# Moving PSUM copies from VectorE to ScalarE in the first eight head pairs, and the decay table's trip through DRAM to the front of the queue

## The chip, the cores and the metric

The kernel runs on one core of a Trainium2 chip. The core has five engines that run side by side and wait for each other by semaphores: TensorE (PE: matrix products and transposes, results in PSUM), VectorE (DVE), ScalarE (ACT), GpSimd (POOL) and SyncE (SP, which here only issues DMAs). The metric is device microseconds per execution. Before the change the median of three runs is 807.27 us (802.27 to 809.57).

## The reference, cut to what matters

Two blocks follow each other. The first is causal attention with a decay over 64 heads (8 batches of 8) of 576 tokens and 64 channels. The second takes the heads' outputs side by side as `x` (8 x 576 x 512) through a gated network whose gate mixes tokens.

```python
log_f = np.log(np.clip(f, 0.0001, 1.0))
cum = np.cumsum(log_f, axis=-1)
decay = cum[:, :, :, None] - cum[:, :, None, :]
scores = np.where(causal, -1000000000.0, scale * q @ k.T + decay)
attn = softmax(scores)              # max taken off, sum + 1e-9
x = heads side by side of attn @ v

h = np.maximum(x @ w_in, 0.0)       # u, v are its two halves
v_n = (v - mu) / np.sqrt(var + 1e-06)
v_s = np.einsum('ts,bsd->btd', w_spatial, v_n) + b_spatial[None, :, None]
out = (u * v_s) @ w_out
```

## The kernel before

The work is cut by pairs of heads: 32 pairs, four to a batch (`PPB`). The tokens of a pair are four blocks of 128 and a tail of 64. One pair goes through these steps:

- `prep` (L218) loads q and k (`qk_t`) and the pair's decay rows (`dk` for the four blocks, `dt` for the tail), and GpSimd writes the causal mask into the latter. The decay rows come from a table, `rows_d`, in DRAM: `decay_rows` (L72) computes the table `rt` once at the start for all heads and writes it out at L86; the loads at L229 and L230 read one row of it into all partitions. `prep_v` (L243) loads v.
- `scores` (L263) and `scores_tail` (L302) let TensorE multiply q by k into PSUM banks `sc`, VectorE subtract the decay and take the row minimum of the negated scores (L260, `lowest`, result `nm`), ScalarE take the exponential with the row sum (L291 and L317), VectorE invert the sum (L294, L295) and GpSimd scale the row (L299, L320). The result is the attention matrix, in `tt` and `tl`; odd pairs of the first batch have tiles of their own, `t`, `d`, `d2t`.
- `transposes` (L344) and `transposes_tail` (L356) transpose its blocks on TensorE (L350, L362) into PSUM tiles `tp`. `evac` (L340) copies each finished `tp` to `e` in SBUF: ten copies to a pair, of which every other one is VectorE's. A counter, `nev`, decides: per pair ScalarE takes four 512 or 256 wide and one of the two tail copies, VectorE takes two of 384, two of 128 and the other tail copy (384).
- `attend` (L370) multiplies `e` by v: 28 products in one piece (L378), which wait for all ten copies. ScalarE rounds the result to `xh` (L387), VectorE keeps the remainder `xl` (L388). L417 copies the last 64 columns of `xl` behind those of `xh`.

While pair P is transposed, pair P+1 is scored: the generator `attention` (L394) interleaves them. `load_first` (L130) splits half of w_in, w_spatial and b_spatial into high and low parts at the same time, with 13 DMAs and work on VectorE, ScalarE and GpSimd; `load64` (L112) is the chain for the weights: `w` loaded, ACT L118, DVE L119, L121, L122, L124, L125, POOL L126, ACT L127, POOL L128. The rest of the weights (`load_rest`, L158) is split inside the first batch's network. `moe` (L431) is the network of one batch: its products are recorded under L214. From the first network on, the main loop (L569 to L577) interleaves the network of a batch with the attention of the next batch.

The order on each engine is not the order of the code: the framework's scheduler rearranges all instructions by its own forecast, within the data dependencies. `after` (L107) adds an ordering edge to that: a DMA is queued on SP behind a marked instruction, without waiting for its end. Before the change the w_in chunks stand behind the first q/k load, and w_spatial and b_spatial behind ScalarE's rounding of the first pair's result (L387), where that is already recorded.

## Time and profile before

| | |
|---|---|
| median of three runs | 807.27 us |
| the profiled execution | 811.62 us, span 809.4 us |
| TensorE busy | 770.3 us (95%) |
| VectorE, ScalarE, GpSimd busy | 444.0, 406.9, 385.6 us |
| mean granted TensorE clock | 0.978 |
| DMA, mean | 98 GB/s |

A row of the timeline gives start and duration, engine, source line, operation, output and input, and in brackets the idle time before it and what ended that. A row of a group gives the count, the total and the mean duration. A window gives the busy time of every engine in a stretch and the clock that was granted to TensorE there (1.00 is full). The 2.2 us between span and execution lie outside the instructions.

### The profile page before, as it was taken

What the parts mean: (1) busy time and instruction counts of PE and PEld (TensorE: products, weight loads), DVE (VectorE), ACT (ScalarE), POOL (GpSimd) and SP (SyncE); (2) the same over time, 40 slices, a digit from 0 to 9 for tenths busy, and PEclk for the clock granted to TensorE, in tenths of its full rate; (3) what the DMA queues carried; (4) which work ended last, traced back from release to release, by engine and by line L of the source; (5) the groups of instructions that cost most, each with busy time, mean ns of one, the idle gap of its engine ahead of it and who ended that gap; (6) DMA issues with size and microseconds to landing.
All of it is one profiled execution on the core that took longest, in us unless ns stands there. A gap on an engine that the chain in (4) does not pass through costs nothing.

```text
span 809.4 us, 14544 instructions
## 1 busy us (share of the span) xinstructions
PE 770.3 (95%) x4933; PEld 608.0 (75%) x4934; DVE 444.0 (55%) x1502; ACT 406.9 (50%) x1100; POOL 385.6 (48%) x713
## 2 busy tenths in 40 slices
PE   8679879899999989999999999999999999999997
PEld 3246668687887867878788877877788877878896
DVE  7866798844654535555564545445454436543322
ACT  3656566554655445555564455544564436542331
POOL 5854676754734236444452437443544435433231
PEclk9879999899999999999999999999999999999999
DMA  8553432434222233333321342222333333201001
GB/s 262 178 158 118 144 131 84 119 108 121 95 95 92 53 112 95 95 108 96 115 92 40 103 134 96 95 92 54 98 95 95 121 105 97 65 27 44 27 1 66
DMA packets 34764, 79.43 MB, mean 98 GB/s; under 512 B 4225, under 2 KB 8321, under 8 KB 34690
## 3 DMA queue, kind: packets, MB, share of 16 engines
q1 hardware_dynamic: 34370, 77.98, 31.2%
q8 instruction: 39, 0.64, 0.4%
q10 hardware_dynamic: 320, 0.52, 0.2%
q14 instruction: 35, 0.29, 0.1%
HBM read 68.73 MB, written 9.75 MB: 97 GB/s over the span
## 4 chain that ended last, share of the span: by engine, by line
PE 71%; DMA 4%; ACT 2%; issue 1%; POOL 1%; DVE 1%; SPq 0%; ACTq 0%; POOLq 0%
PE ps L214 41%; PE sc L378 7%; PE sc L278 7%; PE tp L350 7%; PE sc L214 5%; DMA out_dram<-o 3%; PE tp L214 2%; PE tp L362 1%; ACT o L538 1%; ACT tt L291 1%; DMA dt<-rows_d 0%; POOL tt L299 0%; DVE tt L260 0%; DVE tl L260 0%; POOL gl L514 0%
## 5 line engine op out<-in xcount | busy, mean ns | idle before, releaser
L291 ACT ACTIVATE tt<-tt,nm 128x384 f32<-128x384 f32 (+2 forms) x240 | 133.6, 558 | 93.9 <-DVE nm L260 90.1
L299 POOL TENSOR_SCALAR tt<-tt,sm 128x128 f32<-128x128 f32 x240 | 125.8, 546 | 99.5 <-DVE sm L295 98.7
L514 POOL TENSOR_TENSOR gl<-u,gh 128x256 fp32r<-128x256 f32 (+1 forms) x64 | 51.6, 807 | 142.7 <-ACT gh L513 130.7
L350 PE MATMUL tp<-ident,tt 128*128 128x128 f32 x600 | 105.5, 280 | 4.2 <-ACT e L341 2.6
L378 PE MATMUL sc<-e,vraw 128*64 128x320 f32 (+4 forms) x896 | 97.9, 372 | 6.0 <-ACT e L341 4.3
L350 PEld LDWEIGHTS tp<-ident,tt 128*128 128x128 f32 x600 | 73.4, 141 | 36.2 <-issue 6.8
L378 PEld LDWEIGHTS sc<-e,vraw 128*64 128x64 f32 x896 | 62.1, 141 | 43.9 <-issue 6.4
L341 ACT COPY e<-tp 128x256 f32<-128x256 f32 (+1 forms) x160 | 71.6, 451 | 44.0 <-PE tp L350 40.8
L260 DVE CUSTOM_DVE_ANT_1 tt<-sc,dk 128x256 f32<-128x256 f32 (+1 forms) x120 | 66.0, 551 | 49.6 <-PE sc L278 36.4
L278 PE MATMUL sc<-qk_t 64*128 64x128 f32 (+3 forms) x512 | 89.2, 467 | 3.2 <-DVE nm L260 3.2
L341 DVE COPY e<-tp 128x384 f32<-128x384 f32 (+1 forms) x160 | 70.6, 443 | 29.3 <-PE tp L362 15.0
L214 PE MATMUL ps<-sph,vnh 128*128 128x256 f32 (+1 forms) x240 | 76.1, 317 | 1.3 <-ACT o L538 0.7
L214 PE MATMUL ps<-xh,winh 128*128 128x256 f32 (+1 forms) x232 | 75.2, 324 | 1.7 <-DVE vx L459 1.2
L214 PE MATMUL ps<-spl,vnh 128*128 128x256 f32 (+1 forms) x240 | 71.6, 298 | 0.0
L214 PE MATMUL ps<-sph,vnl 128*128 128x256 f32 (+1 forms) x240 | 71.1, 296 | 0.0
L214 PE MATMUL ps<-xh,winl 128*128 128x256 f32 (+1 forms) x232 | 70.2, 303 | 0.0
L388 DVE TENSOR_TENSOR xl<-sc,xh 128x256 fp32r<-128x256 f32 x64 | 28.8, 453 | 74.9 <-ACT xh L387 74.9
L214 PE MATMUL ps<-xl,winh 128*128 128x256 f32 (+1 forms) x232 | 69.6, 300 | 0.0
L278 PEld LDWEIGHTS sc<-qk_t 64*128 64x128 f32 x512 | 44.7, 189 | 29.6 <-issue 10.3
L214 PE MATMUL ps<-winh,xh 128*128 128x512 f32 x148 | 62.1, 420 | 3.3 <-ACT o L538 3.3
L214 PE MATMUL ps<-winl,xh 128*128 128x512 f32 x148 | 58.5, 396 | 0.0
L260 DVE CUSTOM_DVE_ANT_0 tt<-sc,dk 128x128 f32<-128x128 f32 (+1 forms) x120 | 49.7, 418 | 15.7 <-PE sc L278 10.1
(177 smaller groups left out, 1719.5 us busy)
## 6 DMA issues: line engine op xcount, KB each, us to landing
qk_t<-in_dram SPq DMA_DIRECT2D x32, 608.0 KB, 5.4
dk<-rows_d SPq DMA_DIRECT2D x60, 320.0 KB, 4.3
vraw<-in_dram SPq DMA_DIRECT2D x32, 320.0 KB, 3.0
dt<-rows_d SPq DMA_DIRECT2D x60, 144.0 KB, 3.4
out_dram<-o SPq DMA_DIRECT2D x32, 256.0 KB, 2.3
w<-in_dram SPq DMA_DIRECT2D x16, 256.0 KB, 2.8
w<-in_dram SPq DMA_DIRECT2D x4, 512.0 KB, 6.5
d<-rows_d SPq DMA_DIRECT2D x4, 320.0 KB, 6.6
```

Of the source, the lines that this page charges most:

```text
L214: T.matmul(o, l, r, start=st, stop=sp)
L260: return V.tensor_tensor_reduce(out=out, in0=ps, in1=dec, scale=-0.125, scalar=3.0e38, op0=ALU.add, op1=ALU.min, accum_out=acc_)
L278: return lambda: T.matmul(ps[:, c:c + n], qk_t[p, n - 128:n], qk_t[p, 640:640 + n], start=True, stop=True)
L291: last["exp", P, h, i] = A.activation(t, t, AF.Exp, bias=nm[h][:, i:i + 1], scale=-1.0, accum_out=sm[h][:, i:i + 1])
L299: G.tensor_scalar(out=t, in0=t, scalar1=sm[h][:, i:i + 1], scalar2=1.0, op0=ALU.mult, op1=ALU.mult)
L341: copied.setdefault(P, []).append((V.tensor_copy if nev[0] % 2 == 1 else A.copy)(out, ps))
L350: T.transpose(out=tp[:, (i - c) * 128:(i - c + 1) * 128], in_=tt[h][:, TOFF[i] + 128 * c:TOFF[i] + 128 * c + 128], identity=ident)
L362: T.transpose(out=tp[:, j * 128:(j + 1) * 128], in_=tl[:, c * 128:(c + 1) * 128], identity=ident)
L378: return lambda: T.matmul(x[64 * h:64 * h + 64, q0 - s0:q1 - s0], vt[:, c, h, :], e[:, h, e0 + q0:e0 + q1], start=c == 0, stop=c == end)
L388: freed[s0 // 256] = V.tensor_tensor(out=xl[:, s0:s0 + n], in0=ps[:, 0:n], in1=f32(xh[:, s0:s0 + n]), op=ALU.subtract)
L514: G.tensor_tensor(out=gl[j][:, 0:nt], in0=g, in1=f32(gh[j][:, 0:nt]), op=ALU.subtract)
L538: A.copy(o, ps)
```

## The change

Four edits:

1. `evac` uses VectorE only from the ninth pair on (`P >= 2 * PPB`); in pairs 0 to 7 ScalarE makes all ten copies. 40 copies move.
2. L417's copy of 64 columns goes to ScalarE, for all 32 pairs.
3. On the SP queue the q/k load of the second pair, the loads of w_spatial and b_spatial and each pair's v load are ordered behind the loads of `dk`. The first w_in chunk loses its mark. So the table's write to DRAM no longer stands behind q/k of the second pair, the first piece of w_spatial and v.
4. In `prep` both `dk` loads are issued before the two `dt` loads.

```diff
-        SY.dma_start(out=rows_d[:], in_=rt)
+        last['rows'] = SY.dma_start(out=rows_d[:], in_=rt)
...
-            load64(win_v[:, c, DM:2 * DM, :], winh[:, c, DM:2 * DM], winl[:, c, DM:2 * DM], raw, w[:], t[:], ("dma", 0))
+            load64(win_v[:, c, DM:2 * DM, :], winh[:, c, DM:2 * DM], winl[:, c, DM:2 * DM], raw, w[:], t[:],
+                   None if c == 0 else ("dma", 0))
...
-            after(SY.dma_start(out=raw, in_=w_sp[c * 128:(c + 1) * 128, :]), (0, 0))
+            after(SY.dma_start(out=raw, in_=w_sp[c * 128:(c + 1) * 128, :]), ('dk', 1))
...
-            after(SY.dma_start(out=raw[p0:p0 + 64, :], in_=w_sp[TL:S, :]), (0, 1))
+            after(SY.dma_start(out=raw[p0:p0 + 64, :], in_=w_sp[TL:S, :]), ('dk', 1))
...
-        after(SY.dma_start(out=br, in_=b_sp), (0, 1))
+        after(SY.dma_start(out=br, in_=b_sp), ('dk', 1))
...
         last['dma', P] = SY.dma_start(out=qk_t, in_=qk[P])
+        if P == 1:
+            after(last['dma', P], ('dk', 0))
...
         for h in range(2):
-            SY.dma_start(out=dk[h][:, 0:640], in_=row_of(P, h, 0, 640, 128))
+            last['dk', P] = SY.dma_start(out=dk[h][:, 0:640], in_=row_of(P, h, 0, 640, 128))
+        for h in range(2):
             SY.dma_start(out=dt[64 * h:64 * h + 64, :], in_=row_of(P, h, 640, S, 64))
...
-        SY.dma_start(out=vraw, in_=v[P])
+        after(SY.dma_start(out=vraw, in_=v[P]), ('dk', P))
...
-        copied.setdefault(P, []).append((V.tensor_copy if nev[0] % 2 == 1 else A.copy)(out, ps))
+        copied.setdefault(P, []).append((V.tensor_copy if nev[0] % 2 == 1 and P >= 2 * PPB else A.copy)(out, ps))
...
-            V.tensor_copy(xh[:, S:640], f32(xl[:, TL:S]))
+            A.copy(xh[:, S:640], f32(xl[:, TL:S]))
```

New lines shift the numbers by up to four: L260 becomes L264, L341 becomes L345, L417 becomes L421.

The scheduler's order changes with the edits on every engine; on TensorE it differs from the first transposes to about two thirds of the program, and is the same after that. Three places matter here. The first is the head of the SP queue. Before (`qk_t_280` and `vraw_278` are the second pair's q/k and the first pair's v, `w64` weights, `wraw` w_spatial, `dk_113` and `dk_114` the first pair's decay rows):

```order
L114 DMA w64_251<-in_3_dram 128x1024
L221 DMA qk_t_280<-in_0_dram 128x1216
L140 DMA wraw_460<-in_4_dram 128x576
L245 DMA vraw_278<-in_1_dram 128x640
L86 DMA rows_d_73<-rt_102 64x1216
L114 DMA w64_344<-in_3_dram 128x1024
L229 DMA dk_113<-rows_d_73 128x640
L230 DMA dt_115<-rows_d_73 64x576
L229 DMA dk_114<-rows_d_73 128x640
```

The same place now:

```order
L114 DMA w64_251<-in_3_dram 128x1024
L86 DMA rows_d_73<-rt_102 64x1216
L232 DMA dk_113<-rows_d_73 128x640
L232 DMA dk_114<-rows_d_73 128x640
L234 DMA dt_115<-rows_d_73 64x576 x2
L249 DMA vraw_278<-in_1_dram 128x640
L222 DMA qk_t_280<-in_0_dram 128x1216
L232 DMA d20_282<-rows_d_73 128x640
L232 DMA d21_283<-rows_d_73 128x640
```

The table's write has moved ahead of three loads, and both `dk` loads ahead of `dt`; the third and fourth weight chunk and w_spatial now stand behind the second pair's rows.

The second place is ScalarE just ahead of the first pair's `attend`. `e_312` is the first pair's copied matrix, `t21_360` the second pair's scores, `sc_444` the first pair's result. Before:

```order
L127 CAST winh_74<-w32_412 128x512
L291 ACTIVATE t21_360,sm_364<-t21_360,nm_362 128x512
L341 COPY e_312<-tp_326 128x512
L341 COPY e_312<-tp_337 128x256
L341 COPY e_312<-tp_407 128x2x2x64
L387 CAST xh_442<-sc_444 128x256
```

The same place now:

```order
L295 ACTIVATE t21_360,sm_364<-t21_360,nm_362 128x512
L148 CAST spta_80<-wraw_679 128x576
L127 CAST winh_74<-w32_345 128x512
L345 COPY e_312<-tp_326 128x512
L153 CAST bs0_685<-br_684 1x576
L345 COPY e_312<-tp_332 128x384
L345 COPY e_312<-tp_337 128x256
L345 COPY e_312<-tp_341 128x128
L345 COPY e_312<-tp_407 128x2x2x64
L127 CAST winh_74<-w32_412 128x512
L345 COPY e_312<-tp_424 128x3x2x64
L391 CAST xh_442<-sc_444 128x256
```

Three copies of the first pair have come over from VectorE, and work on w_spatial, b_spatial and two weight chunks has moved between and ahead of the copies.

The third place is VectorE behind the first pair's `attend`, where the third pair's scores (`tt0_82`, `tt1_83`) begin. Before:

```order
L388 TENSOR_TENSOR xl_443<-sc_444,xh_442 128x256
L341 COPY e_503<-tp_505 128x384
L388 TENSOR_TENSOR xl_443<-sc_445,xh_442 128x320
L341 COPY e_503<-tp_514 128x128
L417 CAST xh_442<-xl_443 128x64
L260 ISA tt0_82,nm_539<-sc_545,dk_473 128x384
```

The same place now:

```order
L149 TENSOR_TENSOR sptb_81<-wraw_679,spta_80 64x576
L154 TENSOR_TENSOR bs1_686<-br_684,bs0_685 1x576
L392 TENSOR_TENSOR xl_443<-sc_444,xh_442 128x256
L392 TENSOR_TENSOR xl_443<-sc_445,xh_442 128x320
L264 ISA tt0_82,nm_539<-sc_545,dk_473 128x384
```

L417 and the copies have gone from in front of the scores, and the last pieces of w_spatial and b_spatial have come ahead of `xl`.

## The prediction

> **What bounds the kernel now.** I read the busy times first, then the span cut into four stages at the first pair's `attend` (40.6 us), the first network product (88.9) and the point from which TensorE hardly waits (165). The columns of a window are its limits and length, then busy time (and count) of PE, PEld, DVE, ACT and POOL, the granted clock, the DMA share and GB/s.
>
> ```profile
> PE 770.3 (95%) x4933; PEld 608.0 (75%) x4934; DVE 444.0 (55%) x1502; ACT 406.9 (50%) x1100; POOL 385.6 (48%) x713
> 0.00:40.60 40.60, 29.23 (x123) 13.26 (x124) 30.79 (x85) 22.09 (x54) 27.71 (x51) 0.92 0.69 220
> 40.60:88.90 48.30, 38.82 (x245) 25.16 (x244) 32.79 (x115) 27.72 (x83) 26.50 (x51) 0.82 0.50 156
> 88.90:165.00 76.10, 67.78 (x417) 52.93 (x414) 65.80 (x195) 44.07 (x125) 54.76 (x89) 0.93 0.36 107
> 165.00:809.40 644.40, 634.43 (x4157) 516.61 (x4155) 314.62 (x1109) 312.99 (x839) 276.61 (x525) 1.00 0.28 85
> ```
>
> From 165 us on TensorE is busy 634.4 of 644.4 us at full clock, and no edit takes a product away. What can be won lies ahead of 165 us: TensorE idles 11.4 us in the first stage, 9.5 in the second and 8.3 in the third, and a clock of 0.82 and 0.93 costs up to 8.7 and 5.3 us more in the latter two. Who ends TensorE's waits there:
>
> ```profile
> PE sc L214 <- DVE nm L260: 12.1, 7, 3.1
> PE sc L378 <- ACT e L341: 4.3, 2, 2.3
> PE sc L278 <- DVE nm L260: 3.2, 2, 1.7
> PE tp L350 <- ACT e L341: 2.3, 2, 1.6
> ```
>
> VectorE's row minimum ends 15.3 us of waits (it frees the score banks), ScalarE's copies 6.6. The change takes work from the first and gives it to the second.
>
> **Part 1: L417 and the stall in the second stage.** The timeline at the first long wait, and the three later `attend` pieces:
>
> ```profile
> 45.20 5.06 DVE L417 CAST xh<-xl 128x64 fp32r<-128x64 f32 x1
> 47.41 2.80 POOL L142 TENSOR_TENSOR spl<-wraw,sph 128x576 fp32r<-128x576 f32 x2
> 50.18 0.54 DVE L260 CUSTOM_DVE_ANT_0 tt<-sc,dk 128x384 f32<-128x384 f32 x1
> 50.78 2.29 PE L214 MATMUL sc<-qk_t 128*128 128x288 f32 x4 [3.11 <-DVE nm L260]
> 58.12 5.60 PE L378 MATMUL sc<-e,vraw 128*64 128x320 f32 x28 [1.78 <-ACT tt L291]
> 72.53 2.92 PE L378 MATMUL sc<-e,vraw 128*64 128x320 f32 x28 [2.00 <-ACT e L341]
> 84.43 4.56 PE L378 MATMUL sc<-e,vraw 128*64 128x320 f32 x28 [2.27 <-ACT e L341]
> ...
> L417 DVE CAST xh<-xl x32: 179/194/5059, 45.2 to 756.7; 128x64 fp32r<-128x64 f32 x32
> ...
> 58.00:62.00 4.00, 3.88 (x18) 2.37 (x20) 1.27 (x8) 0.30 (x3) 2.86 (x6) 0.50 0.83 239
> ```
>
> One copy of median 0.19 us lasts 5.06 and ends when GpSimd's run of L142 ends. VectorE's scores come behind it, TensorE idles 3.11 us, and from 58 to 62 us its clock still is 0.50: the same 28 products take 5.60 us at 58.12 and 2.92 at 72.53. On ScalarE the 64 columns can no longer hold up VectorE's queue. The bounds are 0 (the wait comes back elsewhere) and 3.11 + 2.68 = 5.8 us; I take -5.8 for the stall itself, because L417 stands directly in front of L260 before and is gone from there now.
>
> [...]
>
> [...]
>
> **Part 2: the decay rows' way at the head.**
>
> ```profile
> 7.26 0.48 SPq L86 DMA_DIRECT2D rows_d<-rt  x1
> 13.35 0.33 SPq L229 DMA_DIRECT2D dk<-rows_d  x1
> 17.66 0.52 SPq L114 DMA_DIRECT2D w<-in_dram  x1
> 18.98 0.54 DVE L260 CUSTOM_DVE_ANT_0 tt<-sc,dk 128x384 f32<-128x384 f32 x1
> 24.36 1.27 POOL L126 TENSOR_TENSOR w<-w,wa 128x512 f32<-128x512 f32 x1
> 25.30 0.67 ACT L118 ACTIVATE wa<-w 128x512 f32<-128x512 f32 x1 [0.74 <-DMA w<-in_dram]
> 30.15 0.62 ACT L291 ACTIVATE t<-t,nm 128x384 f32<-128x384 f32 x1 [1.01 <-DVE nm L260]
> 7.00:30.00 23.00, 16.22 (x71) 7.20 (x69) 19.38 (x45) 10.54 (x26) 15.12 (x21) 0.85 0.82 244
> ...
> qk_t<-in_dram SPq DMA_DIRECT2D x32, 608.0 KB, 5.4
> vraw<-in_dram SPq DMA_DIRECT2D x32, 320.0 KB, 3.0
> wraw<-in_dram SPq DMA_DIRECT2D x4, 288.0 KB, 8.0
> ```
>
> The write of the table waits for `rt`, not for SP: it was issued at 7.26 and landed 6.0 us later, when the first `dk` load went out, behind q/k (608 KB), w_spatial (288) and v (320). At the 244 GB/s of this stretch these 1216 KB are 5.1 us; as they were partly through by 7.26, I take 3 us. So `dk` can be asked for at about 10.3, and the first row minimum can start 3 to 4 us ahead of 18.98.
>
> But VectorE was busy 19.4 of 23 us there, with the weight chain that the wait let through. That work now comes behind the scores, and the third and fourth weight chunk stand on SP behind the second pair's q/k and decay rows. The last chunk, issued at 17.66, reached ScalarE at 25.30, 7.6 us later; two chunks and three pieces of w_spatial now arrive behind about as many bytes as that, and ScalarE's queue holds their L118 and L141 ahead of the second pair's exponentials. Counting those rows through (fourth chunk 25.3, three pieces of 288 KB at 1.2 us each to 28.9, then 0.67 us for the last L141), the second pair's exponentials start near 29.6, against 30.15. The lead is used up: -0.5 us, bounds -4 and +2.
>
> **Part 3: ScalarE's queue in front of `attend`.** Durations of the copies:
>
> ```profile
> L341 DVE COPY e<-tp 128x384 f32<-128x384 f32 x96 | 52.8, 550 | 22.3 <-PE tp L362 15.0 <-PE tp L350 7.0
> L341 ACT COPY e<-tp 128x512 f32<-128x512 f32 x64 | 37.1, 580 | 22.3 <-PE tp L350 22.0
> L341 ACT COPY e<-tp 128x256 f32<-128x256 f32 x96 | 35.1, 365 | 21.7 <-PE tp L350 18.8 <-PE tp L362 2.5
> L341 DVE COPY e<-tp 128x128 f32<-128x128 f32 x64 | 18.1, 283 | 7.0 <-PE tp L350 6.8
> ```
>
> No ScalarE copy is 384 or 128 wide; between and below its 580 and 365 ns for 512 and 256 I estimate 0.47 and 0.26 us on a straight line. A pair takes 3 x 0.55 + 2 x 0.283 = 2.2 us from VectorE and gives 3 x 0.47 + 2 x 0.26 = 1.9 us to ScalarE. Over eight pairs that is 17.7 and 15.4 us. L417's 32 copies cost ScalarE about 0.2 us each; from 165 us on, and for the whole program's tail columns, TensorE's 98% covers them (without that cover 6 us).
>
> The first `attend` waits for the most. In the new order ScalarE makes three copies of the second half of the first pair only after the rounding of b_spatial (L152), which needs a load that stood far back, and a fourth weight chunk's L127, which needs GpSimd's L126, behind three L142. Before, these came after the first `attend`, at 40.6 us. The price lies between 0 (they are done in time) and 6: three L142 of 1.4 us and one L126 of 1.27 us make 5.5 us on GpSimd, and the rest is copies. I take +3.
>
> For the next three pairs the last two tail copies run one after the other instead of side by side: 0.47 us a pair at least; with the full 1.9 us a pair the most. I take +0.7 a pair, +2 for three.
>
> **Part 4: the first network.** The rows of VectorE's share there, and where TensorE waits:
>
> ```profile
> L341 DVE COPY e<-tp 128x384 f32<-128x384 f32 x9 | 4.9, 546 | 3.1 <-PE tp L362 2.2 <-PE tp L350 0.9
> L341 DVE COPY e<-tp 128x128 f32<-128x128 f32 x6 | 1.6, 274 | 0.0
> L417 DVE CAST xh<-xl 128x64 fp32r<-128x64 f32 x3 | 1.1, 374 | 0.0
> ...
> 111.20 0.89 PE L214 MATMUL sc<-qk_t 128*128 128x288 f32 x2 [2.74 <-DVE nm L260]
> 116.43 0.42 PE L214 MATMUL ps<-xh,winh 128*128 128x320 f32 x1 [1.18 <-DVE vx L459]
> ...
> 112.00:116.00 4.00, 3.26 (x16) 2.89 (x14) 3.97 (x13) 3.32 (x9) 3.32 (x5) 0.61 0.38 111
> 156.00:160.00 4.00, 3.22 (x9) 1.65 (x10) 3.58 (x13) 2.85 (x12) 1.48 (x3) 0.51 0.00 0
> ```
>
> VectorE is busy 65.8 of 76.1 us here, next to fully where TensorE waits for it. 4.9 + 1.6 + 1.1 = 7.6 us leave it; ScalarE, at 44.1 of 76.1, has room for the 9 x 0.47 + 6 x 0.26 + 3 x 0.2 = 6.4 that arrive. The two waits are 3.9 us, the low clock after them 0.39 x 4 = 1.6, that near 156 us 0.49 x 4 = 2.0. The bounds are -7.6 and, if all that arrives on ScalarE fell on TensorE, +6.4. I take -5, two thirds of the relief: the row minima no longer queue behind copies.
>
> **The sum** against the profiled execution: 811.6 - 5.8 - 0.5 + 3 + 2 - 5 = 805.3 us. That execution is 1.0054 times the median of the runs; so 801 us.
>
> **Rivals.**
>
> *Slower: ScalarE's queue becomes the bound of the first two stages.* For it: `attend` already waits 4.3 us for ScalarE's copies, and GpSimd's L142 and L126 now stand ahead of the scaling of the second half of the first pair. If the first `attend` starts after about 44 us instead of 40.6, TensorE idles over 3 us ahead of it and its 28 products run at half clock: then -5.8 shrinks to -3.1 (the clock's loss only moves), the first `attend` costs +6, the pairs +3, and the copies in the network +5 of their 6.4: 811.6 + 10.9 - 0.5 = 822, by the median 818. Against it: ScalarE is busy only 27.7 of 48.3 us in the second stage. Chance 0.19.
>
> *Faster on all terms.* The first `attend` is not later (0), the pairs lose 1, the network wins 7, the head 1: 811.6 - 5.8 - 1 + 1 - 7 = 798.8, by the median 794.5. For it: every wait named goes by VectorE. Chance 0.22.
>
> *It is hidden.* The network's 8.3 us of idling are the order's, not VectorE's, and part 1 and part 3 cancel: 807. For it: from 165 us on nothing can be won, and a scheduler's new order moves waits about. Chance 0.14.
>
> **The numbers.** 0.45 is left for 801 us, with 796 to 806 as its own range. 1% (8.1 us) is about what can be told from no change here: under 799.2 is faster, over 815.3 slower. Faster: the rival's 0.22 and 0.14 of the forecast's lower part, 0.36. Slower: 0.19 and 0.02 for more of the same, 0.21. The same: 0.43. The range 791 to 814 leaves out most of the slower case and the tail of the faster one, about 2 in 10.
>
> **What would show it.** Right: no VectorE copy of over 1 us behind `xl`; clock 1.00 from 50 to 62 us; the second `attend` under 3.2 us; the waits for `nm` in the first 165 us at under 8 us instead of 15.3; the first network product before 88 us. Wrong in part 3: the first `attend` after 44 us with a wait for ScalarE ahead of it. Wrong in part 4: waits of `tp` or `sc` for `e` of over 4 us between 89 and 165 us. Wrong altogether: TensorE idle after 165 us at well over the present 10 us, which would be the new order's own.

## The result, and the profile after

The kernel after takes 816.59 us (median of 4 runs, 815.26 to 817.72), the kernel before 807.76 us beside it (802.27 to 809.57); the ratio is 1.0124, 95% interval 1.0095 to 1.0153. By the ratio it is slower by 10 us (by these two medians 8.8), where 801 us were forecast, and it lies above the range's end of 814. The profiled execution of the kernel after took 816.12 us, half a microsecond under its median; that of the kernel before, 811.62 us, is no typical one: none of its runs in the experiments below reached it (highest 811.08 us, medians of 805.4 to 807.1). The spans of the two profiles (809.4 and 814.0 us) therefore differ by only 4.6 of the 10 us.

The page's busy times, the same four windows, and who ended TensorE's waits in the first 170 us, after:

```profile
PE 772.7 (95%) x4934; PEld 610.8 (75%) x4934; DVE 415.9 (51%) x1430; ACT 424.0 (52%) x1172; POOL 386.8 (48%) x713
0.00:40.60 40.60, 26.78 (x108) 13.06 (x108) 27.93 (x81) 22.82 (x56) 23.82 (x43) 0.87 0.80 242
40.60:88.90 48.30, 39.07 (x235) 24.83 (x237) 22.47 (x92) 32.08 (x103) 27.94 (x53) 0.82 0.38 114
88.90:165.00 76.10, 68.04 (x427) 51.99 (x423) 56.05 (x175) 46.49 (x138) 53.02 (x85) 0.94 0.37 114
165.00:814.00 649.00, 638.81 (x4169) 520.90 (x4169) 309.46 (x1085) 322.59 (x877) 282.05 (x534) 0.99 0.28 85
...
PE tp L354 <- POOL tt L303: 9.7, 5, 4.5
PE sc L382 <- ACT e L345: 8.7, 4, 2.9
PE sc L282 <- DVE nm L264: 6.8, 1, 6.8
PE tp L354 <- ACT e L345: 3.4, 4, 1.3
...
PE sc L215 <- DVE nm L264: 1.2, 2, 1.0
```

The work did move: VectorE is busy 22.5 instead of 32.8 us in the second stage and 56.1 instead of 65.8 in the third, and the many waits for its minima went (`sc` of the tail's products 12.1 to 1.2 us). But one wait of 6.8 us for a minimum has come, GpSimd's scaled scores `tt`, 0.3 us of waits before, now end 9.7 us, and ScalarE's `e` ends 8.7 us in front of `attend`, where it was 4.3 (6.1 with the one wait there for an exponential). L417's copy, now L421 on ScalarE, takes 0.25 us each time:

```profile
L421 ACT CAST xh<-xl x32: 244/245/268, 52.4 to 761.3; 128x64 fp32r<-128x64 f32 x32
```

The timeline's `attend` pieces (start, duration, products, and the wait ahead of them) after:

```profile
45.40 5.39 PE L382 MATMUL sc<-e,vraw 128*64 128x320 f32 x28 [0.72 <-ACT e L345]
60.00 4.61 PE L382 MATMUL sc<-e,vraw 128*64 128x320 f32 x28 [2.50 <-ACT e L345]
73.93 4.61 PE L382 MATMUL sc<-e,vraw 128*64 128x320 f32 x28 [2.60 <-ACT e L345]
88.13 2.19 PE L382 MATMUL sc<-e,vraw 128*64 128x320 f32 x8 [2.87 <-ACT e L345]
...
146.30 2.92 PE L382 MATMUL sc<-e,vraw 128*64 128x320 f32 x28
169.42 4.83 PE L382 MATMUL sc<-e,vraw 128*64 128x320 f32 x28
```

The first `attend` starts 4.8 us later than the 40.58 us of before, the fourth 3.7 us later, the seventh 3.7 us later. The row of the fourth is cut off at 8 of its 28 products; all 28 take 4.52 us. The piece at 146.30 us takes 2.92 us at a granted clock of 1.00 (146 to 150 us). Each of the first four runs for a part at half clock: the granted clock is 0.50 from 46 to 50, from 62 to 64 and from 88 to 90 us, and 0.58 and 0.56 on the mean from 74 to 76 and 76 to 78.

Since most runs below change the order of the work, I compare them by time lost: TensorE's busy time times its granted clock, added up over windows of 2 us, is 753 to 757 us for every kernel; time less this sum is what was lost until a given amount of TensorE's work was done. The columns are about the first `attend` (28 us of work), the fourth (55), the sixth (110), just behind the seventh (130), and the end (752). The sums are good to some 2 us. Each row is one execution, though, and two executions of one program end 5.5 us (before) and 6.9 us (tail_only) apart; so a difference between two rows counts only where more rows agree with it or the ratio bears it out. The names are those of the experiments:

```
time lost, us          28     55    110    130    752   ratio to before, 95% interval
before               13.3   26.2   36.8   42.7   48.4   first profile
before_again         13.7   22.5   33.3   39.4   42.9   second profile of before
tail_only            17.6   24.3   34.0   37.2   40.8   1.0001 (0.9975 to 1.0026)
tail_again           15.9   24.1   36.8   42.8   47.7   second profile of tail_only
loads_only           20.9   31.0   39.6   45.6   50.7   1.0046 (1.0022 to 1.0070)
no_copies            22.1   32.5   41.2   46.0   50.7   1.0032 (1.0006 to 1.0057)
copies_only          19.1   33.3   40.7   51.8   54.1   1.0087 (1.0058 to 1.0116)
after                22.4   34.9   41.5   52.9   55.2   1.0124 (1.0095 to 1.0153)
after_paced          21.9   34.2   42.6   48.9   51.1   1.0086 (1.0058 to 1.0114)
before_paced         15.9   24.2   36.9   43.2   46.3   1.0028 (1.0005 to 1.0050)
first4               22.3   34.5   42.9   48.0   50.1   1.0068 (1.0039 to 1.0098)
tail_alternate       22.3   31.7   41.0   49.2   51.4   1.0116 (1.0078 to 1.0155)
spl_back             18.6   30.6   38.5   42.8   47.4   1.0028 (1.0004 to 1.0051)
weights_late         12.6   25.5   34.4   40.5   42.6   0.9989 (0.9955 to 1.0023)
spl_vector           15.6   28.7   38.1   42.4   44.7   1.0004 (0.9972 to 1.0036)
spl_vector_copies    13.5   30.7   46.3   50.4   52.1   1.0102 (1.0056 to 1.0149)
late_copies          11.8   28.6   36.0   48.0   51.0   1.0060 (1.0036 to 1.0084)
late_copies_paced    12.1   29.9   38.6   45.1   47.9   1.0042 (1.0015 to 1.0068)
late_copies_paced2   12.6   27.5   36.2   41.5   46.8   1.0026 (0.9996 to 1.0055)
```

### The profile page after: what moved, and what is told of

Its sections match the earlier page's. It is cut to its first block, busy times and chain, and to the rows that moved or that the text cites. A ratio compares the mean times of both kernels' runs of the same rounds, so it can differ in the third digit from the quotient of the medians.

```text
span 814.0 us, 14558 instructions
## 1 busy us (share of the span) xinstructions
PE 772.7 (95%) x4934; PEld 610.8 (75%) x4934; DVE 415.9 (51%) x1430; ACT 424.0 (52%) x1172; POOL 386.8 (48%) x713
## 4 chain that ended last, share of the span: by engine, by line
PE 71%; issue 4%; POOL 2%; ACT 2%; DMA 1%; DVE 1%; POOLq 0%; ACTq 0%
PE ps L215 40%; PE sc L382 9%; PE tp L354 7%; PE sc L282 7%; PE sc L215 5%; PE tp L215 2%; PE tp L366 1%; POOL tt L303 1%; DMA out_dram<-o 1%; ACT tt L295 1%; POOL gl L518 1%; DVE tt L264 0%; ACT gh L517 0%; ACT o L542 0%; POOL wol L128 0%
## 5 line engine op out<-in xcount | busy, mean ns | idle before, releaser
L295 ACT ACTIVATE tt<-tt,nm 128x128 f32<-128x128 f32 (+2 forms) x240 | 133.9, 559 | 87.0 <-DVE nm L264 84.8
L354 PE MATMUL tp<-ident,tt 128*128 128x128 f32 x600 | 110.3, 284 | 14.2 <-POOL tt L303 9.7
L354 PEld LDWEIGHTS tp<-ident,tt 128*128 128x128 f32 x600 | 75.2, 143 | 49.2 <-POOL tt L303 15.4
L382 PE MATMUL sc<-e,vraw 128*64 128x320 f32 (+4 forms) x896 | 103.0, 385 | 8.7 <-ACT e L345 8.7
L345 ACT COPY e<-tp 128x256 f32<-128x256 f32 (+1 forms) x200 | 85.6, 441 | 37.2 <-PE tp L354 33.2
L264 DVE CUSTOM_DVE_ANT_1 tt<-sc,dk 128x256 f32<-128x256 f32 (+1 forms) x120 | 66.0, 551 | 54.8 <-PE sc L282 39.8
L345 DVE COPY e<-tp 128x384 f32<-128x384 f32 (+1 forms) x120 | 53.4, 445 | 24.1 <-PE tp L354 15.6
L264 DVE CUSTOM_DVE_ANT_0 tt<-sc,dk 128x128 f32<-128x128 f32 (+1 forms) x120 | 49.9, 419 | 23.5 <-PE sc L282 14.4
```

The source lines that it names most:

```text
L264: return V.tensor_tensor_reduce(out=out, in0=ps, in1=dec, scale=-0.125, scalar=3.0e38, op0=ALU.add, op1=ALU.min, accum_out=acc_)
L295: last["exp", P, h, i] = A.activation(t, t, AF.Exp, bias=nm[h][:, i:i + 1], scale=-1.0, accum_out=sm[h][:, i:i + 1])
L345: copied.setdefault(P, []).append((V.tensor_copy if nev[0] % 2 == 1 and P >= 2 * PPB else A.copy)(out, ps))
L354: T.transpose(out=tp[:, (i - c) * 128:(i - c + 1) * 128], in_=tt[h][:, TOFF[i] + 128 * c:TOFF[i] + 128 * c + 128], identity=ident)
L382: return lambda: T.matmul(x[64 * h:64 * h + 64, q0 - s0:q1 - s0], vt[:, c, h, :], e[:, h, e0 + q0:e0 + q1], start=c == 0, stop=c == end)
```

## The experiments

**One edit at a time.** For the experiments the change falls into three edits: the copies of transposed blocks (evac, the first of the list above), L417's tail copy (the second), and the loads' order (the third and fourth). My theory after the result, Q, was the rival of the prediction: the copies overload ScalarE's queue. Its rivals were L, the loads' new order, and O, that any new order of the instructions costs as much. Three runs take one edit alone and one leaves one out.

```diff
 copies_only: the kernel before, and
-        ... (V.tensor_copy if nev[0] % 2 == 1 else A.copy)(out, ps))
+        ... (V.tensor_copy if nev[0] % 2 == 1 and P >= 2 * PPB else A.copy)(out, ps))
 tail_only: the kernel before, and
-            V.tensor_copy(xh[:, S:640], f32(xl[:, TL:S]))
+            A.copy(xh[:, S:640], f32(xl[:, TL:S]))
 loads_only: the kernel after without these two
 no_copies: the kernel after without the first
```

> The kernel before with one of the three edits: ScalarE makes all copies of transposed blocks of the first eight pairs; the tail copy of L417 stays on VectorE and the loads keep their order. Theory Q (the copies in ScalarE's queue are the cause): the whole loss of about 9 us shows here, a median near 815 us, and TensorE's waits of `sc` for ScalarE's `e` in front of the first four `attend` pieces grow from 4.3 us to about 8. Theory L (the loads' new order is the cause: GpSimd's and ScalarE's weight work in front of the first pairs): this kernel is at or below the kernel before, 800 to 808 us, because VectorE's relief (waits of `nm` in the first 165 us well below 15.3 us) has no counterpart. Theory O (a new order of instructions costs about as much whatever the edit): 810 to 816 us, with the waits spread.

> The kernel before with only L417's copy of 64 columns moved to ScalarE; TensorE's order is that of before. If the stall of 5.06 us on VectorE was worth what I took (3.11 us of idling and 2.68 us of half clock at the second `attend`): 802 us by the median, and the second `attend` lasts 2.9 instead of 5.6 us. If the wait only comes back at another instruction (another VectorE instruction is caught by GpSimd's L142, or ScalarE's copy is late): 806 to 808 us and no VectorE instruction over 1 us would be the sign of the second, another one of 2 to 5 us that of the first. Theories Q, L and O have no price in it but O, which expects no more than 2 us either way since hardly an instruction moves.

> The kernel before with only the loads' edits: decay rows ahead of the second pair's q and k, of v and of the w_spatial and b_spatial pieces, both heads' `dk` ahead of `dt`; all copies stay where they were. Theory Q: no loss, 804 to 808 us, perhaps a gain of the 0.5 us that I gave this part. Theory L: most of the loss of 9 us, 812 to 816 us, with the first `attend` at 43 us or later (40.6 before) although ScalarE has no copy more than before, since GpSimd's L142 and L126 stand ahead of the scaling of the second head. Theory O: 810 to 816 us.

> The kernel after with one edit taken back: the copies of transposed blocks alternate between VectorE and ScalarE in the first eight pairs too; L417 on ScalarE and the loads in the new order stay. Theory Q: the loss is gone, 800 to 806 us, and the first four `attend` pieces start at or before the times of the kernel before (40.6, 58.1, 72.5, 84.4 us). Theory L: the loss stays, 813 to 818 us, with the first `attend` after 43 us. Theory O: 810 to 816 us.

Measured against 806.45 us: copies_only 813.09 us, tail_only 805.61, loads_only 810.34, no_copies 808.33. By the ratios the copies cost 7.0 us, the loads 3.7 us and the tail copy nothing; their sum of 10.7 us is the change's 10.0. So no theory had it alone: Q names the larger part, L the smaller. O is weakened, not refuted: its 810 to 816 us hold for copies_only and loads_only and miss no_copies, and tail_only moves too few instructions to test it; against it speaks that the costs add up. The table shows where, against before_again. The loads lose 7 us by the first `attend`, 8.5 by the fourth, and win 2 of these back by the sixth. The copies lose 5 us more by the first (19.1 against 13.7; tail_only, which costs nothing, has 17.6 there, so a part of it can be the execution's), 5 between the first and the fourth (14.2 against 8.8), win 3 between the fourth and the sixth (7.4 against 10.8), and lose 5 from there past the seventh (11.1 against 6.1). The last step is the firmest: copies_only, after and late_copies (below) lose 11.1 to 12.0 us there, the ten profiles in which VectorE makes its share of the copies 3.2 to 6.3.

**Was the stall the kernel's?** Two kernels were profiled a second time, unchanged.

> The kernel before, profiled once more. If the stall of 5.06 us behind L417 belongs to the kernel: L417's copy behind the first `attend` again lasts 3 us or more and the second `attend` starts 17 us after the first. If it was that one execution's: L417 lasts about 0.2 us there, the second `attend` starts 12.5 to 13.5 us after the first, the fourth at 80 to 82.5 us, and the stretch between the head and the fourth `attend` is 2 to 4 us shorter than in the first profile.

> The kernel before with L417 alone on ScalarE, profiled once more, since its first profile was of its fastest execution. If the stall's end is worth its 5.8 us in each execution: 802 to 804 us, the second to fourth `attend` again 12 to 13 us apart and of 2.9 us each, and the kernel before must have lost the stall in its median execution. If the half clock of the second stage comes and goes by itself: 805 to 809 us, with one or more of the first four `attend` pieces at 4 us or longer though no VectorE instruction lasts over 1 us there.

The timeline of the kernel before in its second profile (806.36 us), `attend` pieces and what stands behind the first:

```profile
41.17 2.93 PE L378 MATMUL sc<-e,vraw 128*64 128x320 f32 x28
53.76 4.61 PE L378 MATMUL sc<-e,vraw 128*64 128x320 f32 x28 [2.19 <-ACT tl L317]
68.02 4.53 PE L378 MATMUL sc<-e,vraw 128*64 128x320 f32 x28 [2.46 <-ACT e L341]
81.52 4.61 PE L378 MATMUL sc<-e,vraw 128*64 128x320 f32 x28 [2.26 <-ACT e L341]
...
45.80 0.32 DVE L417 CAST xh<-xl 128x64 fp32r<-128x64 f32 x1
...
45.94 0.45 POOL L233 TENSOR_SCALAR_AFFINE_SELECT d<-d 128x256 f32<-128x256 f32 x1
...
46.72 4.14 POOL L142 TENSOR_TENSOR spl<-wraw,sph 128x576 fp32r<-128x576 f32 x3
```

GpSimd in the first profile, where the copy started at 45.20 us and took 5.06:

```profile
45.31 0.45 POOL L233 TENSOR_SCALAR_AFFINE_SELECT d<-d 128x256 f32<-128x256 f32 x1
...
46.04 4.16 POOL L142 TENSOR_TENSOR spl<-wraw,sph 128x576 fp32r<-128x576 f32 x3
```

It was that one execution's. The same copy lasts 0.32 us here, although it meets GpSimd as before: in both profiles it starts 0.1 us ahead of a GpSimd select (in the first, GpSimd runs on from there to 50.2 without a gap), and here it gets through. The second `attend` starts 12.6 us after the first instead of 17.5. In the three other profiles with this copy on VectorE at that place it lasts 0.18 to 0.37 us (before_paced, copies_only, loads_only). Of the 5.5 us between the losses of the two profiles, 4.1 arise between the first and the fourth `attend`, where the stall was.

And tail_only against itself, the second to fourth `attend` of the first profile (802.17 us):

```profile
55.62 2.92 PE L378 MATMUL sc<-e,vraw 128*64 128x320 f32 x28 [2.18 <-ACT tl L317]
67.72 2.93 PE L378 MATMUL sc<-e,vraw 128*64 128x320 f32 x28 [2.00 <-ACT e L341]
79.62 2.93 PE L378 MATMUL sc<-e,vraw 128*64 128x320 f32 x28 [2.26 <-ACT e L341]
```

and of the second (808.59 us):

```profile
54.97 4.61 PE L378 MATMUL sc<-e,vraw 128*64 128x320 f32 x28 [2.19 <-ACT tl L317]
68.30 4.61 PE L378 MATMUL sc<-e,vraw 128*64 128x320 f32 x28 [2.00 <-ACT e L341]
81.88 4.61 PE L378 MATMUL sc<-e,vraw 128*64 128x320 f32 x28 [2.27 <-ACT e L341]
```

The program and the waits are the same, the clock is not: after a wait of 2.0 to 2.3 us `attend` runs at full clock in one execution (granted 1.00 from 55 to 86 us) and for the most part at half clock in the other (0.50 from 56 to 58, 69 to 72 and 83 to 85 us). So the full clock of tail_only's first profile proves nothing for the edit either.

**TensorE's order at the seventh `attend`.** This is TensorE's order from the sixth to the seventh `attend`, as kinds of products and their number (`tr` blocks that are transposed, `sc` scores, `sp` w_spatial's and `wo` w_out's products of the network; one `sc` is two products in the profile's rows):

```
before         attend tr4 sp18 tr3 sc6 tr7 sc3 tr3 wo4 sc1 wo2 tr5 wo4 tr2 wo4 attend
after          attend tr6 sp21 tr2 sc6 tr5 sc1 tr5 sc3 tr8 attend
after_paced    attend sp3 tr7 sc6 tr10 sc3 tr3 wo4 sc1 wo2 tr5 wo4 tr4 attend
before_paced   attend tr7 sc6 tr5 sc1 tr5 sc2 tr1 sc1 tr5 wo6 attend
first4         attend tr6 sp17 sc6 tr3 sp14 tr4 sc1 tr5 sc2 tr3 sc1 tr3 wo4 attend
```

The loads' and the tail copy's edit alone leave the order of before there, the copies' edit alone makes that of after. The kernel after's timeline at that place:

```profile
159.74 0.69 PE L354 MATMUL tp<-ident,tt 128*128 128x128 f32 x2 [1.29 <-ACT e L345]
...
164.24 0.55 PE L366 MATMUL tp<-ident,tl 128*128 128x128 f32 x3 [0.45 <-ACT e L345]
168.56 0.93 PE L354 MATMUL tp<-ident,tt 128*128 128x128 f32 x2 [3.77 <-POOL tt L303]
...
163.23 0.33 SPq L232 DMA_DIRECT2D dk<-rows_d  x1
...
167.39 0.41 POOL L237 TENSOR_SCALAR_AFFINE_SELECT dk<-dk 128x256 f32<-128x256 f32 x1 [3.08 <-DMA dk<-rows_d]
...
168.13 0.82 POOL L303 TENSOR_SCALAR tt<-tt,sm 128x128 f32<-128x128 f32 x2
```

Read from the top: TensorE's blocks wait for ScalarE's copies, so the pair's last scores come late, and with them VectorE's last minima, which free `dk`; the next `dk` load goes out at 163.23, GpSimd's select for it stands in front of the scaling of `tt`, and TensorE, with no product of the network in its order there, waits 3.77 us. The two blocks it waits for belong to the next pair, and the new order puts them ahead of `attend`; the last copy that `attend` itself needs ends at 165.85 us. The seventh `attend` then runs at half clock for much of its 4.83 us (granted 0.50 from 168 to 172 us, 0.83 on the mean from 172 to 176). The other two kernels with this order have the same wait (3.19 us in copies_only, 3.75 in late_copies).

Three runs: the kernel after and the kernel before with the second batch's attention emitted a tenth of a batch later, which changes the order from behind the fourth `attend` on, and the kernel after with ScalarE's copies for the first four pairs only.

```diff
 after_paced, before_paced:
-            while da < min(B, b + 1 + LEAD + dm):
+            while da < min(B, b + 1 + (-0.1 if b == 0 else LEAD) + dm):
 first4:
-        ... nev[0] % 2 == 1 and P >= 2 * PPB else A.copy ...
+        ... nev[0] % 2 == 1 and P >= PPB else A.copy ...
```

> The kernel after with one number changed: during the first network the second batch's attention is emitted a tenth of a batch later, so that the scheduler puts 10 of w_out's products (`wo`) between the sixth and the seventh `attend` again, as in the kernel before, where the kernel after has none. All three edits stay, and TensorE's order is untouched through the fourth `attend`. Theory M (the copies' edit costs through TensorE's order at that place: with no products of the network between the tail's transposes and the seventh `attend`, TensorE waits there for GpSimd's scaling and falls to half clock): about 6 us of the loss go, 809 to 811 us, the stretch from 165 to 200 us has TensorE busy 35 us at clock 1.00 (31.4 at 0.90 in the kernel after), and the waits of `tp` for GpSimd's `tt` fall from 9.7 to about 5 us. Theory Q (the copies are too many for ScalarE's queue, whatever TensorE's order): 814 to 818 us, with the waits for ScalarE's `e` and GpSimd's `tt` as long as before, only at other places.

> The kernel before with the same one number changed and none of the three edits: VectorE makes its share of all copies. The scheduler now puts w_out's products behind the transposes ahead of the seventh `attend` (none among the scores and the tail's blocks, six at the very end). Theory M: this alone costs what the copies' edit cost, 811 to 814 us, with TensorE idle 3 us or more and below full clock between 155 and 180 us. Theory Q: no loss, 804 to 808 us, since ScalarE has no copy more than in the kernel before.

> The kernel after with ScalarE's copies kept for the first four pairs only; from the fifth pair on VectorE makes its share as before. In the new order w_out's products still stand late, four of them directly ahead of the seventh `attend` and none among the scores. Theory M: the loss stays for the most part, 812 to 816 us, although ScalarE is relieved exactly where the kernel after waits. Theory Q (the copies of the fifth to eighth pair fall on TensorE): the 6 to 7 us between 150 and 175 us are gone, 808 to 810 us. A third reading, that the first four pairs' copies are the loss (rival Slower of the prediction): 814 to 817 us with waits for `e` of 8 us or more ahead of the first four `attend` pieces, and full clock from 165 us on.

The stretch from 165 to 200 us, in the kernel after:

```profile
165.00:200.00 35.00, 31.44 (x193) 24.20 (x193) 14.22 (x54) 17.42 (x49) 20.95 (x40) 0.90 0.37 111
```

in after_paced:

```profile
165.00:200.00 35.00, 34.46 (x226) 26.87 (x225) 16.38 (x62) 19.28 (x57) 19.86 (x39) 1.00 0.41 125
```

Measured 811.66, 808.74 and 811.58 us against 805.4. In after_paced the loss at the place is gone as M said (6.3 us between the sixth and behind the seventh, 11.4 in the kernel after), but the total falls by 3 us and not 6; a part comes up earlier. before_paced refutes M in its pure form: with VectorE's share of the copies, and no product of the network among the scores and blocks but six directly ahead of `attend`, the place costs 6.3 us as ever, and the whole 2.2 us. first4 says much the same: four such products directly ahead of `attend`, copies shared, 5.1 us there. But in neither do blocks of the next pair stand ahead of `attend` behind the tail's blocks, as the two do in the kernel after. So the kernels that lose 5 us more at this place have three things together: ScalarE alone behind the blocks, no product of the network there, and the next pair's two blocks ahead of `attend`. after_paced, with blocks of the next pair ahead of `attend` too (0.54 us of waiting), shows that products of the network can cover it; which of the other two is needed, these runs do not separate.

**The head.** What the loads' edit does to it, in the kernel after's timeline of SP, VectorE, ScalarE, TensorE and GpSimd:

```profile
10.46 0.81 SPq L232 DMA_DIRECT2D dk<-rows_d  x2
...
18.00 0.81 SPq L114 DMA_DIRECT2D w<-in_dram  x2
...
14.62 0.56 DVE L264 CUSTOM_DVE_ANT_0 tt<-sc,dk 128x384 f32<-128x384 f32 x1 [1.04 <-POOL dk L237]
...
21.06 0.68 DVE L264 CUSTOM_DVE_ANT_1 tt<-sc,dk 128x512 f32<-128x512 f32 x1
26.20 0.43 DVE L119 TENSOR_SCALAR wa<-wa 128x512 f32<-128x512 f32 x1 [4.45 <-ACT wa L118]
26.54 0.68 DVE L264 CUSTOM_DVE_ANT_1 tt<-sc,dk 128x512 f32<-128x512 f32 x1
...
25.50 0.66 ACT L118 ACTIVATE wa<-w 128x512 f32<-128x512 f32 x1 [5.26 <-DMA w<-in_dram]
...
27.29 2.93 PE L282 MATMUL sc<-qk_t 64*128 64x384 f32 x12 [6.77 <-DVE nm L264]
...
39.52 1.92 PE L354 MATMUL tp<-ident,tt 128*128 128x128 f32 x6 [4.46 <-POOL tt L303]
...
31.64 1.84 POOL L143 TENSOR_TENSOR spl<-wraw,sph 128x576 fp32r<-128x576 f32 x1
...
37.32 1.79 POOL L126 TENSOR_TENSOR w<-w,wa 128x512 f32<-128x512 f32 x1
39.09 2.55 POOL L303 TENSOR_SCALAR tt<-tt,sm 128x128 f32<-128x128 f32 x4
```

The first minimum does come 4.4 us earlier (14.62 against 18.98). `dk` is asked for at 10.46 us, as I had worked out (10.3). But the third and fourth weight chunk leave at 18.00 us (the third at 11.96 in before_again); the third arrives at 25.5 us and has its L119 in VectorE's order ahead of the pair's last minimum, and TensorE waits 6.77 us for that minimum; then three L143 and an L126 stand on GpSimd ahead of the second head's scaling, and TensorE waits 4.46 us more. Two runs take these out of the way, with VectorE's share of the copies:

```diff
 spl_back: no_copies, and w_spatial and b_spatial where they were
-            after(SY.dma_start(out=raw, in_=w_sp[c * 128:(c + 1) * 128, :]), ('dk', 1))
+            after(SY.dma_start(out=raw, in_=w_sp[c * 128:(c + 1) * 128, :]), (0, 0))
 ... (its last rows and b_sp likewise, (0, 1))
 weights_late: spl_back, and in load_first
-                   None if c == 0 else ("dma", 0))
+                   None if c == 0 else ("dma", 0) if c == 1 else ("exp", 0, 1, 3))
```

> Loads' edit in part, L417 on ScalarE, copies as in the kernel before: w_spatial and b_spatial take their old places behind the second pair's scores again, the decay rows still go ahead of the second pair's q and k and of v. GpSimd's order has the eight scalings of the first pair ahead of all L143 and L126 again, and VectorE has both 512-wide minima of the first pair ahead of the third weight chunk's L119. Theory H (the loads' edit costs at the head, 3.7 us as measured alone, because weight work that came late stands ahead of the first pair's minimum on VectorE, 6.8 us of waiting at 27 us, and ahead of its scaling on GpSimd, 4.8 us at 39 us): both waits go, the first `attend` starts at 41 us or before instead of 44.5, and the median falls by 3 to 5 us from 808.3 to 803 to 805. Rival (the loss is in the loads themselves, decay rows and q and k arriving later for the second pair): the first `attend` stays after 43.5 us and the median at 807 to 809 us.

> As in the run before it in this call (w_spatial and b_spatial in their old places), and the third and fourth weight chunk are ordered behind the first pair's exponentials too, so that L119 and L126 of both stand behind the second pair's first minima and behind the first pair's scaling. Theory H: as good or better than that run, the first `attend` at 38 to 40.5 us, 801 to 805 us; the four us of lead of the first row minimum (14.6 instead of 18.9 us) arrive at the first `attend` for the first time. Rival (the first network then lacks its weights or VectorE and ScalarE do the weight chain later at the same price): the first `attend` is early, but the second to fourth or the network from 82 us on give it back, 806 to 809 us.

spl_back: first `attend` at 41.59 us, 3 us earlier than in no_copies (44.54), but 807.06 us, no gain that the intervals show; between the first and the fourth `attend` it loses 12.0 us against 10.4. Of the two waits the first shrinks from 6.77 to 2.73 us, but one of 4.61 us for `tt` is still there: GpSimd now waits 3.31 us for a `dt` load ahead of the scaling. weights_late: first `attend` at 36.52 us, the earliest up to here, and 805.46 us, a ratio of 0.9989 against 1.0032 for no_copies, with intervals that just overlap. So H is borne out for what holds up the first `attend`; that this is also the loss in time is likely, not shown. Its 3 to 5 us did not come from the first of the two runs, and the lead of 4.7 us over before_again is gone by the second `attend`, as its rival said. The timeline of weights_late there:

```profile
47.80 3.51 DVE L320 TENSOR_TENSOR nm<-nm 128x1 f32<-128x1 f32 x1
...
45.94 4.13 POOL L143 TENSOR_TENSOR spl<-wraw,sph 128x576 fp32r<-128x576 f32 x3
50.04 1.25 POOL L128 TENSOR_TENSOR winl<-w,winh 128x512 fp32r<-128x512 f32 x1
...
53.86 4.42 PE L382 MATMUL sc<-e,vraw 128*64 128x320 f32 x28 [5.50 <-ACT e L345]
```

A minimum over two columns takes 3.51 us and ends when GpSimd's run ends, at 51.3 us. It looks like the stall of L417 again, on another instruction. The next run takes L143 off GpSimd:

```diff
-            G.tensor_tensor(out=spl[:, c, :], in0=raw, in1=f32(sph[:, c, :]), op=ALU.subtract)
+            V.tensor_tensor(out=spl[:, c, :], in0=raw, in1=f32(sph[:, c, :]), op=ALU.subtract)
```

> The kernel of the run with the late weights (decay rows first, third and fourth weight chunk behind the first pair's exponentials, copies as in the kernel before, L417's copy on ScalarE), and the four subtractions of L143 go from GpSimd to VectorE. In the run with the late weights the first `attend` starts at 36.5 us, 4.7 us ahead of the kernel before's second profile, and the second starts no earlier (53.9 against 53.8 us): VectorE's minimum of one column, L320, lasts 3.51 us there, beside GpSimd's three L143 and one L128. Theory G (a VectorE instruction that works on SBUF alone stands still while GpSimd works through a run of such subtractions, whichever instruction it is that meets them; so the stall of L417 was moved and not removed): without L143 on GpSimd no small VectorE instruction lasts over 2 us between 40 and 60 us, the second `attend` starts at 48 to 50.5 us, and the median is 797 to 802 us. Rival (the second `attend` waits for the pair's loads or for ScalarE in any case): second `attend` after 52.5 us, 804 to 807 us.

807.91 us, and the second `attend` at 56.32 us: no gain. The small instructions no longer stand still (L320 takes 0.15 us there), but one L143 on VectorE itself takes 2.44 us and another 1.35, ahead of the minima. Theory G's stall is seen in two profiles, but its price of 3 to 8 us was not to be had this way; where the lead goes without any such work between 40 and 50 us was not tried.

**The copies alone.** tail_alternate gives VectorE the last tail copy back; the other three put all copies on ScalarE into kernels with the mended head, the last two of them with another pace.

```diff
 tail_alternate: the kernel after, and
-        ... and P >= 2 * PPB else A.copy ...
+        ... and (P >= 2 * PPB or out.shape[-1] == 64) else A.copy ...
 spl_vector_copies, late_copies: spl_vector and weights_late with the copies' edit
 late_copies_paced, late_copies_paced2: late_copies, and
-            while da < min(B, b + 1 + LEAD + dm):
+            while da < min(B, b + 1 + (-0.1 if b == 0 else LEAD) + dm):      (-0.05 in the second)
```

> The kernel after, but VectorE makes the last tail copy of each of the first eight pairs again (the 384 columns directly ahead of `attend`, five blocks of eight stay ScalarE's); all other copies stay on ScalarE. Theory Q in its narrow form (two tail copies one after the other on ScalarE lengthen the wait in front of each `attend` by 0.5 to 0.6 us, to 2.5 to 2.9 us, and so surely halve the clock at each of the first four): these waits fall to about 2.0 us, the fourth `attend` starts 2 to 5 us before 88.1 us, and the order now has ten of w_out's products ahead of the seventh `attend`, so that this loss goes too; 808 to 812 us. Theory H alone (the head is the loss): 815 to 817 us.

> The same kernel, and ScalarE makes all copies of the first eight pairs. In this order 18 and more of w_out's products stand ahead of the seventh `attend`, so that TensorE has the network's work there. Theory Q with M (the copies cost through ScalarE's serial tail copies ahead of each `attend` and through TensorE's order at the seventh): the first part stays, the second goes, 2 to 4 us slower than the run before it in this call, with over 95% of TensorE busy at clock 1.00 from 165 to 200 us. If the copies' edit costs its 7 us whatever the order: 6 to 8 us slower. If it is a gain once GpSimd and the weights are out of the way (my part 4): up to 5 us faster.

> The kernel after with its head mended alone: w_spatial and b_spatial in their old places and the third and fourth weight chunk behind the first pair's exponentials; ScalarE makes all copies and L417's. TensorE's order has no product of w_out among the scores and tail blocks ahead of the seventh `attend`, as in the kernel after. If the parts add up (head about 3 us of the kernel after's loss, copies 7 us): 811 to 814 us, some 7 us over the run with the late weights (805.5), first `attend` at 36 to 38 us, TensorE below 33 us busy or below clock 0.95 between 165 and 200 us. If the early head gives ScalarE the room that the copies need: 804 to 808 us.

> The kernel of the run with the mended head and all copies on ScalarE (812.0 us), with the second batch's attention emitted a tenth of a batch later during the first network; 10 of w_out's products then stand among the blocks ahead of the seventh `attend`, where that run had none. By that run's profile the copies cost next to nothing up to 150 us and 6 us between 150 and 175 us. Theory M (the copies' loss is TensorE's order there): those 6 us go, 805 to 807.5 us, level with the same kernel without the copies (805.5). Rival (ScalarE's copies cost 6 us wherever they stand, the waits only move ahead of 150 us, as 3 us of them did when the kernel after was paced the same way): 809 to 812 us.

> The same with a twentieth of a batch in place of a tenth: 16 of w_out's products stand ahead of the seventh `attend`, behind its pair's first tail block. Theory M: as the run before it, 804 to 808 us. Rival: 809 to 812 us. If the two runs differ by over 3 us, the order's small details weigh as much as the copies do.

tail_alternate, 813.92 us: in its profile it loses 3 us less from the first to the fourth `attend` (9.4 against 12.5) and 3 less at the seventh, but that is its fastest execution (811.81 us); by the ratio it gains 0.6 us over the kernel after, which the intervals do not show, where Q in its narrow form expected 808 to 812 us. It has ten of w_out's products ahead of the seventh `attend`, and still waits 2.59 us there for a scaled block of the next pair and loses 8.2 us: products of the network alone do not cover the place. late_copies, 811.96 us: the parts add up (0.7% over weights_late, 5.7 us). Up to the sixth `attend` the copies cost it 1.6 us, there 6 (12.0 against 6.1). The two paced kernels lose 6.5 and 5.3 us there, as those without the copies, and take 808.6 and 807.81 us; they gain 3.4 and 4.2 us by their medians, 1.5 and 2.7 by the ratios, whose intervals overlap. spl_vector_copies has w_out's products at that place and loses 4.1 us there, but 15.6 between the fourth and the sixth (spl_vector 9.4), and takes 815.11 us: the cost has moved ahead. So a part of the copies' cost, a quarter to a half by the ratios (1.5, 2.7 and, with after_paced, 3.1 us, each with intervals that overlap), seems to go with TensorE's order at the seventh `attend`; the rest is not tied to one place by these runs. No kernel here beats the kernel before by more than can be measured.

## Why the prediction was wrong

Three steps failed. Part 1's -5.8 us measures 0. Part 2's -0.5 measures +3.7, because a wait behind a weight chunk on VectorE was not in it. Parts 3 and 4, +5 and -5, cancelled in the sum, and the copies cost +7.0: the relief of VectorE was over-sized, and the wait for the scaled `tt` at the seventh `attend` was in no term. These misses of 5.8, 4.2 and 7.0 us are about the way from -6 us to +10.

*Part 1, -5.8 us: the step that failed first.* The size of the stall was about right for that execution: the two profiles of the kernel before differ by 5.3 us of span, and 4.1 us of lost time arise where the stall was. The half clock at the second `attend`, 2.68 us of the term, was not the stall's alone: before_again has no stall, and its second `attend` takes 4.61 us, at a granted clock of 0.56 from 54 to 56 us and 0.59 from 56 to 58. And the stall was one execution's (5.06 us for the copy, 0.32 in before_again), and I divided the sum by 1.0054 to come to the median, as if all of its terms were in every execution. Against the median the term is 0, and tail_only measures 0 (1.0001). Of its signs one held, no VectorE copy of over 1 us stands behind `xl`; the second `attend` takes 4.61 us, the clock from 50 to 62 us is 0.93 on the mean, and the waits for `nm` are 8.0 us, just at the bound.

*Part 2, -0.5 us, bounds -4 and +2: measured +3.7 (1.8 to 5.6), above the bound but for the interval's low end.* The loads were counted nearly rightly: `dk` at 10.46 us (10.3 forecast), the table's write landing in 3.1 us instead of 6.0, the third chunk's L118 at 25.50 and the fourth's at 27.53 (25.3 for the fourth), the second pair's exponentials at 30.74 (29.6). What was not looked at is where the third chunk's L119 stands in VectorE's order: ahead of the first pair's own last minimum, not behind it. I spoke of ScalarE's queue and the second pair; the wait came on VectorE, for the first.

*Part 3, +3 for the first `attend` and +2 for the next three.* The first `attend` came at 45.40, past the 44 us given as the sign of an error, 4.2 us behind before_again. Only 1.7 us of these are there with the copies alone (copies_only 42.87); no_copies, with the loads and without the copies, is at 44.54, so most is part 2's. The serial tail copies lengthen the waits ahead of the next three by 0.1 to 0.6 us, to 2.50, 2.60 and 2.87, less than the 0.7 taken; but from the first to the fourth `attend` the copies cost 5 us in copies_only against before_again, where I had 2; in the kernel after against no_copies they cost 2.1 us there. Which of the two is the rule, these single profiles do not say.

*Part 4, -5 us.* The relief is there and was over-sized: VectorE is busy 9.8 us less in the third stage, the minima's waits are gone, and 4 us less are lost between the fourth and the sixth `attend` (6.6 against 10.8; 2 of the 4 are there in no_copies too, 8.7), although the first network product comes at 92.58 us, not before 88. Then 5 us more are lost at the seventh, at 165 us, where I had let the account end. The rival Slower priced ScalarE's copies in the network at +5, and the bound of +6.4 held this case; the wait, however, is not one for `e`: those stay at 3.9 us between 89 and 165 us, under my sign of 4. It is one for `tt`, three steps behind them, in a chain through VectorE, a `dk` load and GpSimd.

*The rivals.* Slower is what happened by size (818 forecast, 816.6 measured) and by its first sign. Its mechanism, ScalarE's queue in the first two stages, is only a part of it: the copies lose there, but the head is the weights', and the seventh `attend` was in nobody's sum. "TensorE idle after 165 us well over 10 us" did not occur (10.2). The copies' and the loads' edits are shown to be the cause by the runs with one edit; the path by which the copies cost their 7 us is shown only in part.

## What to carry to other kernels

Before a long wait of one profile becomes a term, see whether it belongs to the order or to one execution: profile the same kernel twice, and do not scale a single event to the median. When a load is moved back, follow every instruction that it feeds to its place in each engine's order, and ask whose minimum or scaling stands behind it. Off-loading an engine wins only as much as the chain behind the new engine is covered; look for the place where TensorE has nothing else in its order.

## What the runs showed of the hardware

In two profiles a small VectorE instruction lasted until a run of GpSimd instructions beside it had ended: 5.06 us for a copy of 64 columns (the first profile of before, 45.20 to 50.26 us; GpSimd's two selects and three L142 end at 50.20), 3.51 us for a minimum over two columns (weights_late, 47.80 to 51.31 us; the L143 and the L128 behind them end at 51.29). The same copy at about the same distance to GpSimd's next instruction took 0.32 us in another execution (before_again). I had taken the stall for a property of the order; what decided between the two executions, whose copies start 0.11 and 0.14 us ahead of the select, the rows do not show. What makes the instruction last so long is not shown by a run either.

A wait of 2.0 to 2.3 us on TensorE is followed by full clock in the first profile of tail_only (`attend` in 2.92 and 2.93 us) and by half clock in the second profile of the same program (4.61 us). 4.61 less 2.92 us are 1.69 us; by estimate that is 3.4 us at half clock. The granted clock of the second profile gives the same: its means over 2 us are 0.77, 0.50 and 0.87 from 54 to 60 us, 0.69, 0.50 and 0.96 from 68 to 74, and 0.60 and 0.55 from 82 to 86, and each of the three comes to 3.4 us at 0.50. What decides between full and half clock after the same wait, these rows do not show.
